# First phase of an adaLN attention and SwiGLU kernel: bias halves summed from PSUM, two zero-weight matmuls in a wait, K's first load between two weight loads

## The chip, the cores and the metric

The kernel runs on one core of one Trainium2 chip. The metric is the device time of one execution in microseconds (us). Each kernel was also profiled: the profile gives the span of the execution (first to last instruction, about 1.8 us shorter than the device time here), the busy time of each engine, and the clock granted to TensorE. Beside the time, each timed execution has its own span and its own mean granted clock, rounded to three decimals.

Engine names in the profile: PE is TensorE's matmuls, PEld its weight loads, DVE VectorE, ACT ScalarE, POOL GpSimd, SPq the queue that issues the loads. L1029 is a line of the kernel's source.

## The reference

```python
mod = (silu(c) @ w_mod)                # six vectors: sa, ca, ga, sb, cb, gb
h = layernorm(x) * (1 + ca) + sa       # x: 2048 x 1024
q = h @ wq                             # 32 heads of 128
s = q @ k.T * Dh ** -0.5               # last 512 keys, 4 kv heads
x = x + ga * (softmax(s) @ v) @ wo     # heads joined before wo
h = layernorm(x) * (1 + cb) + sb
x = x + gb * (silu(h @ w_gate) * (h @ w_up)) @ w_down
```

## The kernel before

The kernel works on blocks of 512 rows. All of the change lies in the first 35 us, where the first block's Q for heads 0 to 6 is made before the shift vector `sa` is there: Q is accumulated from the scaled input alone (`hs`), and what the shift adds to a head's Q, one column of 128 numbers, is made by matmuls whose `rhs` is a single column and added as a bias when Q is read from PSUM, where the kernel keeps the results of its matmuls. (In a matmul, `lhsT` is the weights; the columns of `rhs` are the last number of a timeline shape, 1 or 512.) All of these one-column results lie in one PSUM tile, `one_ps`: row 0 is the shift vector, rows 1 and 2 are the two halves of the bias.

```python
one_ps = mm("one_ps", (P, 3, 8))       # one PSUM tile

def q0(g, dts, src=None):              # Q of head g: matmuls of 512 columns
    for dt in dts:
        nc.tensor.matmul(q0_ps[g], lhsT=w0(g, dt),
                         rhs=hs[dt // 4][:, dt % 4, :] if src is None else src[:, dt, :],
                         start=(dt == 0), stop=(dt == DT - 1))

def sh_mm(half, heads):                # half of the bias: 4 one-column matmuls per head
    ...
            nc.tensor.matmul(one_ps[:, 1 + half, g:g + 1], lhsT=w0(g, dt),
                             rhs=sa_bf[:, dt:dt + 1], start=(i == 0), stop=(i == 3))

def sa_mm(half, tiles):                # shift vector: 8 one-column matmuls per tile
    ...
...
q0(3, (6, 7))
sh_mm(0, range(4))
q0(4, (6, 7))
sh_mm(0, range(4, H0))
...
nc.vector.tensor_copy(out=bias_q, in_=one_ps[:, 1, 0:H0])          # L1083
sa_mm(1, (0, 1))
q0(5, (6, 7))
sa_mm(1, (2, 3))
sa_out(1)                              # DVE reads the shift, casts it to bf16 (sa_bf)
q0(6, (6, 7))
sh_mm(1, range(H0))
...
nc.vector.tensor_tensor(out=bias_q, in0=one_ps[:, 2, 0:H0], in1=bias_q, op=ALU.add)   # L1094
q0_ps[H0] = mm("q_ps")                 # head 7 takes the bank of one_ps
q0(H0, range(DT), h10)
```

The loads go through one queue in program order: x, the modulation weights `wm`, `wq`, then the part that is changed:

```python
load_v(0)
load_wq(0, 2)                          # two loads of 512 KB, first used by head 8
load_kT(0)                             # K of kv head 0, transposed by the DMA
```

## Time and profile before

Three executions took 1273.43 to 1274.11 us, median 1273.8.

The page of the kernel before, its span, its busy times (share of the span, times the instructions) and the shares of the chain of waits that ended last:

```profile
span 1273.1 us, 18160 instructions
PE 1264.5 (99%) x7587; PEld 641.5 (50%) x7587; DVE 610.1 (48%) x1335; ACT 335.6 (26%) x440; POOL 1.3 (0%) x10
PE 97%; DVE 2%; DMA 0%; SPq 0%; issue 0%
```

PE is busy practically all the time and is the chain. So a delay of PE in the first phase is not hidden by anything later; it moves the end.

PE's rows of the timeline in that phase. The columns are start in us, busy us, engine, line, operation, what it writes and reads, shapes, how many, and in brackets how long the engine was idle before and what ended it. Rows of `128x1` are the one-column matmuls, rows of `128x512` the dense ones.

```profile
24.69 0.54 PE L1040 MATMUL one_ps<-sa_bf,wq 128*128 128x1 bf16 x16
25.09 0.59 PE L1029 MATMUL q_ps<-hs,wq 128*128 128x512 bf16 x2
25.52 0.44 PE L1040 MATMUL one_ps<-sa_bf,wq 128*128 128x1 bf16 x12
26.22 0.54 PE L1047 MATMUL one_ps<-siluc,wm 128*128 128x1 bf16 x16 [0.26 <-DVE bias_q L1083]
26.62 0.59 PE L1029 MATMUL q_ps<-hs,wq 128*128 128x512 bf16 x2
27.05 0.54 PE L1047 MATMUL one_ps<-siluc,wm 128*128 128x1 bf16 x16
27.45 0.59 PE L1029 MATMUL q_ps<-hs,wq 128*128 128x512 bf16 x2
28.05 0.84 PE L1040 MATMUL one_ps<-sa_bf,wq 128*128 128x1 bf16 x28
29.14 3.33 PE L1029 MATMUL q_ps<-hT,wq 128*128 128x512 bf16 x8 [0.26 <-DVE bias_q L1094]
32.26 1.32 PE L1190 MATMUL s_ps<-qT,kT 128*128 128x512 bf16 x4
...
36.25 1.07 PE L1222 MATMUL o_ps<-v_sb,pT 128*128 128x130 bf16 x16
```

Three things are to be seen. At 26.22 PE has waited for the DVE copy of the first bias half (L1083). At 29.14 it has waited for the second half (L1094), because head 7's Q takes the bank of `one_ps`. And the eight matmuls after that take 3.33 us, where eight such matmuls take 1.89 us later in the same trace.

The waits view of the window 22 to 32 us has the same two waits (total us, times, longest):

```profile
PE q_ps L1029 <- DVE bias_q L1094: 0.3, 1, 0.3
PE one_ps L1047 <- DVE bias_q L1083: 0.3, 1, 0.3
```

The windows view shows why the eight were slow. Its columns are the stretch, its length, the busy us of PE, PEld, DVE, ACT and POOL with their instructions, the granted clock of TensorE, the DMA share and GB/s:

```profile
22.60:26.02 3.42, 3.36 (x68) 2.25 (x67) 1.64 (x7) 0.00 (x0) 0.00 (x0) 1.00 1.12 325
26.02:29.43 3.41, 2.95 (x66) 2.12 (x66) 1.59 (x7) 1.54 (x3) 0.00 (x0) 1.00 1.95 157
29.43:32.84 3.41, 3.41 (x10) 1.24 (x9) 3.41 (x6) 1.12 (x2) 0.00 (x0) 0.50 1.02 189
32.84:36.26 3.42, 3.39 (x17) 1.37 (x16) 0.36 (x1) 3.08 (x4) 0.00 (x0) 1.00 0.18 50
```

The clock is 1.00, 1.00, then 0.50 for one stretch of 3.41 us, then 1.00 again. The cuts are set where the clock changes, and at multiples of 3.41 us from there.

| read from the profile of before | us |
|---|---|
| span | 1273.1 |
| PE stopped for `bias_q`, twice | 0.26 each |
| half-clock stretch | 29.43 to 32.84 |
| first one-column matmul to first `o_ps` matmul (22.86 to 36.25) | 13.39 |

The last row is the measure used below: it holds everything that the change touches on PE, and nothing of the loads of the start, whose arrival differs by about 1 us between executions (the first one-column matmul of this phase starts at 22.16 us in one trace below, that of real fill, and at 23.27 us in another, the second of before).

### The profile page before, as it was taken

The numbers are of one execution on the slowest core, as the hardware profiler recorded it, in microseconds if no ns is written. First come the engines' busy times: TensorE is split into PE (matmuls) and PEld (weight loads), VectorE is DVE, ScalarE is ACT, GpSimd is POOL, SyncE is SP. The second block draws the span as 40 slices with busy tenths as digits, with TensorE's granted clock in tenths as the row PEclk, the third lists the DMA queues.
The fourth block names the chain that finished last, engine by engine and source line by source line (L and its number), as shares of the span: only waits on it lengthen the run. The fifth ranks groups of instructions, "written<-read, shape, count | busy, mean of one in ns | idle before, by whom it ended". The sixth has DMA issues, their size and how long they took to land.

```text
span 1273.1 us, 18160 instructions
## 1 busy us (share of the span) xinstructions
PE 1264.5 (99%) x7587; PEld 641.5 (50%) x7587; DVE 610.1 (48%) x1335; ACT 335.6 (26%) x440; POOL 1.3 (0%) x10
## 2 busy tenths in 40 slices
PE   8999999999999999999999999999999999999998
PEld 4555555555555555555554444444444444444444
DVE  5666658885678665567564631321122112221122
ACT  3643334343333433334341111011100111011100
POOL 0000000000000000000000000000000000000000
PEclk9999999999999999999999999999999999999999
DMA  9897755878556655454575378326633566425702
GB/s 290 193 242 179 190 141 139 190 161 213 135 141 168 153 135 156 114 153 104 129 199 150 124 225 259 95 92 206 212 116 111 168 201 193 157 91 168 245 17 70
DMA packets 306844, 204.46 MB, mean 161 GB/s; under 512 B 145601, under 2 KB 303297, under 8 KB 306754
## 3 DMA queue, kind: packets, MB, share of 16 engines
q1 hardware_dynamic: 301842, 199.03, 57.8%
q10 hardware_dynamic: 4912, 4.20, 1.0%
q8 instruction: 61, 1.00, 0.3%
q14 instruction: 29, 0.24, 0.1%
HBM read 165.94 MB, written 4.21 MB: 134 GB/s over the span
## 4 chain that ended last, share of the span: by engine, by line
PE 97%; DVE 2%; DMA 0%; SPq 0%; issue 0%
PE gu_ps L1336 30%; PE a_ps L1254 17%; PE q_ps L1179 16%; PE d_ps L1356 15%; PE o_ps L1222 9%; PE s_ps L1190 8%; PE q_ps L1029 1%; DVE st L842 0%; DMA x<-in_A_x_dram 0%; DVE junk L1113 0%; DVE junk L813 0%; DVE oq L1209 0%; DVE qT L943 0%; DVE f L1267 0%; DVE f L1266 0%; DVE x L1269 0%
## 5 line engine op out<-in xcount | busy, mean ns | idle before, releaser
L1192 ACT ACTIVATE pT<-s_ps 128x1024 bf16<-128x1024 f32 x256 | 249.2, 1020 | 346.7 <-PE s_ps L1190 346.6
L1254 PE MATMUL a_ps<-wo,oT 128*128 128x512 bf16 x1024 | 241.9, 379 | 0.0
L1179 PE MATMUL q_ps<-hT,wq 128*128 128x512 bf16 x960 | 227.1, 379 | 0.0
L1342 DVE TENSOR_TENSOR guT<-gu_ps,sg 128x512 bf16<-128x512 f32 x112 | 77.5, 692 | 288.3 <-ACT sg L1341 288.3
L1336 PE MATMUL gu_ps<-hT,wg 128*128 128x512 bf16 x896 | 211.7, 379 | 0.0
L1341 ACT ACTIVATE sg<-gu_ps 128x512 bf16<-128x512 f32 x112 | 67.0, 598 | 488.5 <-PE gu_ps L1336 485.7
L1356 PE MATMUL d_ps<-wd,guT 128*128 128x512 bf16 (+2 forms) x952 | 194.2, 366 | 0.0
L1336 PE MATMUL gu_ps<-hT,wu 128*128 128x512 bf16 x672 | 163.3, 379 | 0.0
L1254 PEld LDWEIGHTS <-oT 128*128 128x128 bf16 x1024 | 100.2, 98 | 120.6
L943 DVE CAST qT<-q_ps 128x512 bf16<-128x512 f32 x121 | 83.6, 691 | 153.2 <-PE q_ps L1179 152.9
L1179 PEld LDWEIGHTS <-wq 128*128 128x128 bf16 x960 | 93.9, 98 | 113.0
L1356 PEld LDWEIGHTS <-guT 128*128 128x128 bf16 x952 | 90.9, 98 | 103.0
L1222 PEld LDWEIGHTS <-pT 128*128 128x128 bf16 x2048 | 126.6, 98 | 30.5 <-issue 0.4
L1336 PEld LDWEIGHTS <-wg 128*128 128x128 bf16 x896 | 87.6, 98 | 105.5
L1222 PE MATMUL o_ps<-v_sb,pT 128*128 128x130 bf16 x2048 | 137.0, 220 | 0.1
L1190 PE MATMUL s_ps<-qT,kT 128*128 128x512 bf16 x512 | 131.8, 380 | 0.0
L1336 PEld LDWEIGHTS <-wu 128*128 128x128 bf16 x672 | 65.7, 98 | 79.3
L1209 DVE TENSOR_TENSOR oq<-o_ps,rl 128x256 bf16<-128x256 f32 (+2 forms) x256 | 100.5, 420 | 3.9
L1360 DVE TENSOR_TENSOR f<-d_ps,gb_bc 128x512 f32<-128x512 f32 (+2 forms) x34 | 22.5, 660 | 140.8 <-PE d_ps L1356 140.8
L1190 PEld LDWEIGHTS <-kT 128*128 128x128 bf16 x512 | 45.1, 98 | 31.7 <-issue 1.3
L1262 DVE TENSOR_TENSOR acc<-a_ps,acc 128x512 f32<-128x512 f32 x64 | 44.0, 688 | 32.6 <-PE a_ps L1254 32.6
L1336 PE MATMUL gu_ps<-hT,v_sb 128*128 128x512 bf16 x224 | 57.5, 379 | 0.0
(97 smaller groups left out, 426.5 us busy)
## 6 DMA issues: line engine op xcount, KB each, us to landing
wq<-in_A_wq_dram SPq DMA_DIRECT2D x64, 512.0 KB
wo<-in_A_wo_dram SPq DMA_DIRECT2D x64, 512.0 KB
wg<-in_B_w_gate_dram SPq DMA_DIRECT2D x56, 512.0 KB
wd<-in_B_w_down_dram SPq DMA_DIRECT2D x56, 512.0 KB
wu<-in_B_w_up_dram SPq DMA_DIRECT2D x42, 512.0 KB
v_sb<-in_B_w_up_dram SPq DMA_DIRECT2D x14, 512.0 KB
x<-in_A_x_dram SPq DMA_DIRECT2D x16, 256.0 KB
wm<-in_w_mod_dram SPq DMA_DIRECT2D x4, 1024.0 KB
```

Of the source, the lines that this page charges most:

```text
L943: nc.vector.tensor_copy(out=t, in_=q_ps)
L1179: nc.tensor.matmul(q_ps, lhsT=w, rhs=hT[("h1", cc)][:, dt, :], start=(dt == 0), stop=(dt == DT - 1))
L1190: nc.tensor.matmul(s_ps[:, i, :], lhsT=kT[:, kv, j * P:(j + 1) * P], rhs=qT[g], start=True, stop=True)
L1192: nc.scalar.activation(out=p[:, 2 * jj:2 * jj + 2, :], in_=s_ps, func=ACT.Exp, scale=scale)
L1209: nc.vector.tensor_tensor(out=dst, in0=ps[:, s0:s0 + cnt, 0:Dh], in1=sc, op=ALU.mult)
L1222: nc.tensor.matmul(o_slot["ps"][:, s_, :], lhsT=pT[g][:, j, t * P:(t + 1) * P], rhs=v_sb[:, kv, j, 0:VN], start=(j == 0), stop=(j == WT - 1))
L1254: nc.tensor.matmul(a_ps, lhsT=oT[(cc, 2 * q + i)][:, hh % 4, t * P:(t + 1) * P], rhs=wo_tiles[(cc, q, dh, i)][:, hh % 4, :], start=(hh == ...
L1262: nc.vector.tensor_tensor(out=acc[(cc, t)][:, dsl], in0=a_ps, in1=acc[(cc, t)][:, dsl], op=ALU.add)
L1336: nc.tensor.matmul(ps[:, n, :], lhsT=gu_w[(cc, fg, nm, dt // 4)][:, dt % 4, fi * P:(fi + 1) * P], rhs=hT[("h2", cc)][:, dt, :], start=(dt ...
L1341: nc.scalar.activation(out=g, in_=ps[:, 0, :], func=ACT.Silu)
L1342: nc.vector.tensor_tensor(out=guT[(cc, fg)][:, fi, :], in0=ps[:, 1, :], in1=g, op=ALU.mult)
L1356: nc.tensor.matmul(d_ps, lhsT=guT[(cc, f // 4)][:, f % 4, t * P:(t + 1) * P], rhs=wd_tiles[(cc, dh, f // 4)][:, f % 4, c0:c0 + w], start=( ...
```

## The change

It means to take PE's two stops away and to keep its clock up. The bias halves are no longer copied one by one: one DVE reduce at the end sums both rows straight from PSUM, so PE need not wait in the middle. The one-column groups are dealt out differently between the dense pairs. Two dense matmuls with weights of zero, which add nothing to head 6's Q, run while DVE makes that sum. And K's first load goes between the two loads of `wq`, since scores will be wanted sooner.

```diff
-    load_wq(0, 2)
+    load_wq(0, 2, (0,))
     load_kT(0)
+    load_wq(0, 2, (1,))
...
+    zeros = const.tile([P, P], BF16, name="zeros")
+    nc.gpsimd.memset(zeros, 0.0)
...
-                             start=(dt == 0), stop=(dt == DT - 1))
+                             start=(dt == 0), stop=(dt == DT - 1 and g != H0 - 1))
...
-    sh_mm(0, range(4))
+    sh_mm(0, range(5))
     q0(4, (6, 7))
-    sh_mm(0, range(4, H0))
+    sh_mm(0, (5, 6))
...
-    nc.vector.tensor_copy(out=bias_q, in_=one_ps[:, 1, 0:H0])
-    sa_mm(1, (0, 1))
+    sa_mm(1, (0,))
     q0(5, (6, 7))
-    sa_mm(1, (2, 3))
+    sa_mm(1, (1, 2, 3))
     sa_out(1)
-    q0(6, (6, 7))
+    q0(H0 - 1, (6,))
+    q0(H0 - 1, (7,))
     sh_mm(1, range(H0))
+
+    for i in range(2):
+        nc.tensor.matmul(q0_ps[H0 - 1], lhsT=zeros, rhs=warm_w, start=False, stop=(i == 1))
...
-    nc.vector.tensor_tensor(out=bias_q, in0=one_ps[:, 2, 0:H0], in1=bias_q, op=ALU.add)
+    nc.vector.tensor_reduce(out=bias_q, in_=one_ps[:, 1:3, 0:H0].rearrange("p a g -> p g a"),
+                            axis=AX.X, op=ALU.add)
```

## The prediction

> **What bounds it.** TensorE. The page gives PE 99% busy over 1273.1 us, and the chain that ended last is 97% PE. From 33 us on the windows view shows PE busy nearly all the time, so what moves the first head's dense work moves the end by as much.
>
> **Where time is lost there (timeline, PE rows).**
> 1. At 25.98 PE stops until 26.22: it may not write `one_ps` before DVE has copied `bias_q` (L1083). The next 16 one-column matmuls take 0.54 us, against 0.38 in the chain elsewhere: 0.24 + 0.16 = 0.40 us.
> 2. At 28.90 it stops until 29.14: the bank that head 7's Q needs is read last by the second `bias_q` (L1094).
> 3. The windows view shows the granted clock at 0.50 in 29.43 to 32.84 and 1.00 around it. 512-column matmuls start there every 0.427 us instead of 0.215; eight lose 8 x 0.21 = 1.7 us. [...] the slow stretch is 3.41 us long, and the equal stretch before it (26.02 to 29.43) is the thinnest: about 1.15 us of 512-column streaming (5.3 x 0.215), against about 1.55 in the stretch before, which kept the clock.
>
> **What the change does.**
> - Bias halves summed straight from PSUM: removes wait 1 (-0.40 us) and a DVE copy of 0.17 us (off the path); the final reduce should take about the 0.17 us of the add it replaces.
> - Two zero matmuls: +0.43 us on PE, into wait 2, where 0.24 us of idle and 0.16 of restart vanish: about 0.
> - Reordering moves one-column work, removes none. Dense streaming starts near 28.5 (zero matmuls), head 7's Q near 28.9. The stretch 26.02 to 29.43 then holds about 1.8 us of streaming, more than the 1.55 that kept the clock. So no half clock: -1.5 to -1.7 us.
> - K's first transpose lands about 30.4 in the trace, and scores started at 32.26. With a faster PE scores want it near 30.65; issued 1.5 us earlier it lands near 29. Worth nothing itself; it keeps the gain from becoming a DMA wait. The second `wq` half lands later, but is first used near 32.5.
> - The zeros memset (POOL) is off the path.
>
> **On the critical path:** 0.2 to 0.4 us of waits and up to 1.7 us of clock, less some 0.2 us because ACT's 0.97 us exponentials pace the first two heads. First `o_ps` matmul at about 34.4 instead of 36.25; the shift stays to the end. Sum: -1.8 us, 0.14%.
>
> **Prediction:** 1272.0 us, range 1270.9 to 1273.3. Faster by over 2%: 0.5%; within 2%: 99%; slower by over 2%: 0.5%.
>
> **What would show it.** Granted clock 1.00 throughout 20 to 40 us; no PE row waiting for `bias_q`; head 7's eight Q matmuls in about 1.9 us instead of 3.33; scores starting near 30.7 without waiting for `kT`.
>
> **What would make it wrong.** [...] in another phase a thin stretch (24.7 to 28.1 holds about 1.3 us even after the change) may still trip it, leaving only 0.3 us; or the timed runs of before did not all pay it. Scores may wait for `kT` or ACT. Run to run noise is 0.7 us, near the effect's size.

-0.40 us for the first wait, about 0 for the zero matmuls, -1.5 to -1.7 us for the clock and some 0.2 us back for ACT came to -1.8 us. The clock term was the estimate from one trace, in which a stretch with 1.15 us of dense work was followed by the half clock and one with 1.55 us was not. In the last paragraph, "another phase" is another place of these 3.41 us stretches, and what a thin stretch may "trip" is the clock.

## The result, and the profile after

The changed kernel took 1272.92 to 1273.72 us, median 1273.02 of 6 executions; the kernel before, 1273.43 to 1274.63, median 1273.98 of 6. The ratio is 0.9993, with a 95% interval of 0.998 to 1.0006. A ratio here is the mean time of one kernel's runs over that of the other's of the same rounds, so it is not quite the ratio of the medians. 0.96 us of 1274 is far under 2%, and the interval holds 1. The profiled span is 1271.2 us, 1.9 us under that of before.

The page after, the lines that answer to those of before:

```profile
span 1271.2 us, 18164 instructions
PE 1263.8 (99%) x7589; PEld 641.3 (50%) x7589; DVE 609.8 (48%) x1334; ACT 335.6 (26%) x440; POOL 1.4 (0%) x11
PE 97%; DVE 2%; DMA 0%; SPq 0%; issue 0%
```

PE's rows of the timeline after (columns as above; L1032 is the dense Q, L1043 the bias, L1050 the shift vector, L1095 the zero matmuls):

```profile
24.80 0.64 PE L1043 MATMUL one_ps<-sa_bf,wq 128*128 128x1 bf16 x20
25.30 0.59 PE L1032 MATMUL q_ps<-hs,wq 128*128 128x512 bf16 x2
25.73 0.34 PE L1043 MATMUL one_ps<-sa_bf,wq 128*128 128x1 bf16 x8
25.93 0.34 PE L1050 MATMUL one_ps<-siluc,wm 128*128 128x1 bf16 x8
26.13 0.59 PE L1032 MATMUL q_ps<-hs,wq 128*128 128x512 bf16 x2
26.56 0.74 PE L1050 MATMUL one_ps<-siluc,wm 128*128 128x1 bf16 x24
27.16 0.59 PE L1032 MATMUL q_ps<-hs,wq 128*128 128x512 bf16 x2
27.76 0.84 PE L1043 MATMUL one_ps<-sa_bf,wq 128*128 128x1 bf16 x28
28.46 0.59 PE L1095 MATMUL q_ps<-warm_w,zeros 128*128 128x512 bf16 x2
28.89 1.89 PE L1032 MATMUL q_ps<-hT,wq 128*128 128x512 bf16 x8
30.61 1.03 PE L1197 MATMUL s_ps<-qT,kT 128*128 128x512 bf16 x4
...
34.31 1.07 PE L1229 MATMUL o_ps<-v_sb,pT 128*128 128x130 bf16 x16
```

No row waits for `bias_q` any more. The zero matmuls start at 28.46, head 7's eight Q matmuls take 1.89 us and not 3.33, and the first `o_ps` matmul starts at 34.31 instead of 36.25. From the first one-column matmul (22.96) to there it is 11.35 us, against 13.39.

The windows view after, cut at multiples of 3.41 us from this execution's first rise of the clock (7.21 us):

```profile
24.27:27.69 3.42, 3.42 (x71) 2.20 (x69) 1.94 (x9) 0.10 (x1) 0.00 (x0) 1.00 1.25 217
27.69:31.10 3.41, 3.41 (x42) 1.92 (x41) 3.09 (x8) 2.57 (x4) 0.00 (x0) 1.00 1.40 186
31.10:34.51 3.41, 3.38 (x19) 1.50 (x18) 1.72 (x3) 3.27 (x4) 0.00 (x0) 1.00 0.71 120
```

The clock is 1.00 in all of them. From the first `o_ps` matmul to the end it is 1236.86 us after and 1236.89 before (span less start): nothing later was gained or lost.

So the two traces differ by 1.97 us of span and agree with the predicted 1.8 almost step by step. The timed medians differ by 0.96 us only. The experiments were made to find where the other half is.

### The profile page after: what moved, and what is told of

Same layout as the page of the kernel before. It is cut to its first block, busy times and chain, and to the rows that moved or that the text cites. A ratio compares the mean times of both kernels' runs of the same rounds, so it can differ in the third digit from the quotient of the medians.

```text
span 1271.2 us, 18164 instructions
## 1 busy us (share of the span) xinstructions
PE 1263.8 (99%) x7589; PEld 641.3 (50%) x7589; DVE 609.8 (48%) x1334; ACT 335.6 (26%) x440; POOL 1.4 (0%) x11
## 4 chain that ended last, share of the span: by engine, by line
PE 97%; DVE 2%; DMA 0%; SPq 0%; issue 0%
PE gu_ps L1343 30%; PE a_ps L1261 17%; PE q_ps L1186 16%; PE d_ps L1363 15%; PE o_ps L1229 9%; PE s_ps L1197 8%; PE q_ps L1032 1%; DVE st L845 0%; DMA x<-in_A_x_dram 0%; DVE junk L1120 0%; DVE junk L816 0%; DVE oq L1216 0%; DVE qT L946 0%; DVE f L1274 0%; DVE f L1273 0%; DVE x L1276 0%
```

## The experiments

Two theories. The clock theory, a guess from the trace of before (3.41 us at clock 0.50 after a stretch of 3.41 us with 1.15 us of dense work): the half clock follows a stretch, from here on a window, of 3.41 us that held too little streaming by dense matmuls; where the windows lie differs from one execution to the next, so the kernel before pays that in a part of its executions, and the changed kernel in none. The waits-only rival: the gain is that of the two stops, and the half clock has nothing to do with what the change does.

"Streaming" below is worked out from the timeline: 0.215 us, the start to start distance of 512-column matmuls at full clock, for each such matmul, as far as it lies in the window; the recorded starts are taken as the starts of streaming. Some records are missing (rows of `x1` where the kernel has pairs); they are added, one each in the windows below of sum alone and of zeros alone. In the traces, 512-column matmuls start 0.427 us apart at half clock and 0.215 us at full clock, one-column matmuls 0.025 us apart.

Mean clocks of 0.998 are read below as executions with one half-clock window in the middle, those of 0.999 or 1.0 as executions without: the trace of before, with one, has 0.998, that of after, without, 1.0. (3.41 us at half clock take 0.0013 from the mean; in these two traces the clock also falls for the last 1.26 and 1.03 us, which takes 0.0005 and 0.0004.) A reading near the edge of rounding can mislead for a single run; for the kernel before the times agree with it: its ten runs with 0.998 took 1274.43 us or more, and of its 31 others one took more than 1274.1 (1274.52).

### The parts alone

**Sum from PSUM alone.**

```diff
-    nc.vector.tensor_copy(out=bias_q, in_=one_ps[:, 1, 0:H0])
...
-    nc.vector.tensor_tensor(out=bias_q, in0=one_ps[:, 2, 0:H0], in1=bias_q, op=ALU.add)
+    nc.vector.tensor_reduce(out=bias_q, in_=one_ps[:, 1:3, 0:H0].rearrange("p a g -> p g a"),
+                            axis=AX.X, op=ALU.add)
```

> Only the first part: the two bias halves are summed by one reduce from PSUM, no copy of the first half; order of before, no zero matmuls, old DMA order. Both theories: the stop of PE at 25.98 us is gone, head 7's Q starts 0.40 us sooner (28.74 instead of 29.14). Clock theory: the stretch before Q stays thin (two pairs of 512-column matmuls and about 0.2 us of a third, 1.1 us of streaming in the thinnest 3.41 us), so half-clock windows still occur in some or most executions: times spread over some 1.5 us, median 0.4 us under before. Waits-only theory (the half clock has nothing to do with the thin stretch): 0.4 us under before, and half-clock windows as often as in the changed kernel.

Measured: 1273.04 to 1274.93, median 1274.07 of 5; before, in the same session, 1272.81 to 1275.06, median 1273.47 of 9. Two of the five runs have clock 0.998, and two of the nine of before. The 0.4 us under before that both theories expected is not seen in the medians, which depend on how many half clocks fell on each side. The trace happened to be one with a half clock: 13.09 us from the first one-column matmul to the first `o_ps` matmul, 0.30 less than the 13.39 of before, also at half clock. The stop in the middle is gone; the expected 0.40 fell short by 0.1, probably because the second half of the shift weights landed only at 26.00 us by the DMA's completion events; PE's next one-column matmul started at 26.05. The windows view:

```profile
25.94:29.35 3.41, 3.07 (x72) 2.24 (x71) 1.65 (x7) 1.62 (x3) 0.00 (x0) 1.00 1.59 137
29.35:32.76 3.41, 3.41 (x10) 1.18 (x8) 3.41 (x6) 1.04 (x2) 0.00 (x0) 0.50 1.50 153
```

The thin window held 1.22 us of streaming and brought the half clock.

**Zero matmuls alone.**

```diff
+    zeros = const.tile([P, P], BF16, name="zeros")
+    nc.gpsimd.memset(zeros, 0.0)
...
     sh_mm(1, range(H0))
+    for i in range(2):
+        nc.tensor.matmul(q0_ps[H0 - 1], lhsT=zeros, rhs=warm_w, start=False, stop=(i == 1))
```

> Only the two zero matmuls, everything else as before. Both theories: PE's stop at 28.90 us is filled; the zero matmuls cost 0.43 us and save 0.24 of idle and 0.16 of restart, so Q of head 7 starts at about 29.33 and ends where it would have at full clock (within 0.05 us). Clock theory: dense streaming starts 0.24 us sooner than in before, the thinnest 3.41 us holds about 1.05 to 1.1 us instead of 0.87: half-clock windows become rarer but do not vanish; median 0.3 to 1 us under before. Waits-only theory: no change of time (within 0.1 us).

Measured: 1273.37 to 1274.99, median 1273.56 of 5; one run has clock 0.998. By time alone, no difference from before that these runs could show; the 0.3 to 1 us that the clock theory expected is not there. The trace is worth more: the clock window fell in the same place as in the run above (25.93), and the clock stayed up:

```profile
25.93:29.35 3.42, 3.08 (x73) 2.21 (x71) 1.52 (x8) 1.34 (x2) 0.00 (x0) 1.00 1.99 188
29.35:32.76 3.41, 3.38 (x17) 1.44 (x16) 3.41 (x6) 2.42 (x5) 0.00 (x0) 1.00 0.95 176
```

PE's busy time in the two thin windows is the same within 0.01 us (3.07 and 3.08); what differs is streaming, 1.22 against 1.34 us, of which 0.43 are the zero matmuls. So matmuls with weights of zero count for the clock as other dense ones do, as far as this trace shows: without them the window would hold 0.91 us, less than the 1.22 us after which the clock fell. At full clock this kernel needs 11.74 us for the measured stretch.

**Everything but the zero matmuls** (the two-line loop taken out of the changed kernel, and the `stop` flag put back).

> The changed kernel without the two zero matmuls (sum from PSUM, new order and new DMA order stay). Both theories: Q of head 7 starts at about 28.75 after a PE stop of 0.24 us and 0.16 us of restart; at full clock the same time as the changed kernel within 0.05 us. Clock theory: the thinnest 3.41 us holds about 1.2 us instead of 1.3 (and 1.2 to 1.3 in a wider range of phases), so some executions have a half-clock window and are 1 to 1.7 us longer; spread over 1 us. Waits-only theory: same times and same spread as the changed kernel.

Measured: 1272.73 to 1274.73, median 1273.39 of 5; one run (the 1274.73) has clock 0.998, the others 0.999 or 1.0. The trace, at full clock, needs 11.31 us, the changed kernel 11.35. So at full clock the zero matmuls gain nothing that can be seen: the difference of 0.04 us is less than that between traces of one kernel (the changed kernel's three need 11.35, 11.36 and 11.48). What they are good for is the clock.

**One-column matmuls in the place of the dense zero ones.**

```diff
-    for i in range(2):
-        nc.tensor.matmul(q0_ps[H0 - 1], lhsT=zeros, rhs=warm_w, start=False, stop=(i == 1))
+    for i in range(17):
+        nc.tensor.matmul(q0_ps[H0 - 1][:, 0:1], lhsT=zeros, rhs=warm_w[:, 0:1], start=False, stop=(i == 16))
```

> The changed kernel with the two 512-column zero matmuls replaced by 17 zero matmuls of one column (17 x 25 ns = 0.43 us): PE is as busy and never stops, but streams 0.43 us less. This separates filling the wait from streaming. Clock theory [...]: dense work starts at 28.9 instead of 28.5, the thinnest 3.41 us holds about 1.1 us, half-clock windows come back in some executions, which are 1 to 1.7 us longer than the others. Waits-only theory: time and spread equal to the changed kernel (within 0.1 us).

Measured: 1272.64 to 1274.93, median 1273.12 of 5; one run (1274.93) has clock 0.998, the others are at 1273.31 or less. The trace, at full clock, needs 11.34 us. Filling the wait costs the same with either kind. With one-column matmuls a half clock still comes, in one run of five.

### The kernel before in another phase, and the changed kernel again

> The kernel before, unaltered, for a trace in another phase of the clock window and for the count of its slow-clock executions. Clock theory: about a quarter of executions have the half clock (clock 0.998, span about 1273.0). If this trace falls in another phase (3 in 4), it shows full clock between 20 and 40 us and the time from the first one-column group to the first o_ps matmul is 11.7 to 11.8 us, not 13.39: 0.4 us over the changed kernel's 11.35, and span about 1271.6. Rival (the half clock belongs to every execution of the kernel before, as my prediction assumed): 13.4 us again and clock 0.998 in all runs.

Measured: 1272.99 to 1274.73, median 1273.57 of 5; one run has clock 0.998 (1274.73). Beside it, in the nine runs of before of that session, two have 0.998 (1275.02 and 1274.97), the other seven are 1273.30 to 1273.66. The trace is one at full clock. Its windows:

```profile
24.20:27.61 3.41, 3.15 (x74) 2.21 (x72) 1.78 (x7) 0.00 (x0) 0.00 (x0) 1.00 1.35 314
27.61:31.03 3.42, 3.16 (x54) 1.89 (x50) 2.64 (x8) 2.67 (x4) 0.00 (x0) 1.00 1.48 106
31.03:34.44 3.41, 3.38 (x16) 1.46 (x15) 2.48 (x4) 2.54 (x3) 0.00 (x0) 1.00 0.86 155
```

And three of PE's rows in it, head 7's Q after the wait, the first scores, the first output:

```profile
29.55 1.89 PE L1029 MATMUL q_ps<-hT,wq 128*128 128x512 bf16 x8 [0.26 <-DVE bias_q L1094]
31.27 1.03 PE L1190 MATMUL s_ps<-qT,kT 128*128 128x512 bf16 x4
...
34.97 1.07 PE L1222 MATMUL o_ps<-v_sb,pT 128*128 128x130 bf16 x16
```

The unaltered kernel before, with both its stops, needs 11.70 us here, not 13.39. The thin window held 1.29 us of streaming and passed. So one form of the rival fails, the one that my prediction shared: the half clock does not belong to every execution of the kernel before.

> The changed kernel again, unaltered, to count its executions with a half-clock window beside the others on the same chip. Clock theory: the thinnest 3.41 us of it holds about 1.3 us of streaming; two traces bracket the threshold (1.22 us tripped, 1.34 us did not), so none or at most one of five runs shows clock 0.998; the rest 1272.6 to 1273.4 us. Waits-only theory: 0.998 as often as in the kernel before (2 of 9 runs in the last session).

Measured: 1272.65 to 1273.33, median 1272.87 of 5, no clock of 0.998. Before in that session: 1273.16 to 1274.76, median 1273.89 of 9, two with 0.998. The trace needs 11.36 us.

> The changed kernel once more, beside the two others on the same chip. No run with clock 0.998; median 1272.7 to 1273.1 us.

Measured: 1272.46 to 1273.77, median 1273.22 of 5, no clock of 0.998. The median is a little over what was expected. The trace needs 11.48 us.

All runs of the two kernels that have a clock of their own, over all sessions (so over several chips):

| | runs | with clock 0.998 | mean of those, us | mean of the others, us |
|---|---|---|---|---|
| before | 41 | 10 | 1274.85 | 1273.49 |
| after | 16 | 0 | - | 1273.04 |

If the clock reading had nothing to do with the change, none in 16 beside 10 in 41 would come about by chance in some 3 of 100 cases. Where the clock stayed up, the change is worth 1273.49 - 1273.04 = 0.45 us (give or take 0.2), about the 0.35 us by which the traces differ at full clock (11.70 against 11.35). An execution of before with a half-clock window is 1.36 us longer than one without. Ten of 41 have one: 0.24 x 1.36 = 0.33 us on the average. The sum, 0.78 us (give or take 0.3), is what the change gains on the average. In the three sessions that ran both kernels the means differ by 0.90, 1.01 and 0.73 us.

### Thin against dense, with the same time on PE

To see the clock without luck, the wait was made much longer than it needs to be, once with one-column matmuls and once with dense ones, each about 2.15 us.

**86 one-column zero matmuls** (as the 17 above, with 86).

> The changed kernel with 86 one-column zero matmuls (86 x 25 ns = 2.15 us) in place of the two of 512 columns: PE issues without a stop but streams almost nothing for 2.8 us. Both theories: 2.15 - 0.43 = 1.72 us more PE time than the changed kernel. Clock theory: nearly every phase of the window now has a thin window, so nearly all five runs show clock 0.998 and are 1.2 to 1.7 us longer still: about 3.0 to 3.4 us over the changed kernel, and as much as 1.2 to 1.7 us over the next kernel. Waits-only theory: equal to the next kernel.

**Ten dense zero matmuls** (`range(10)` in place of `range(2)`).

> The changed kernel with ten 512-column zero matmuls (10 x 0.215 = 2.15 us) in place of two: the same PE time as the run with 86 one-column matmuls, but all of it streaming. Both theories: 1.72 us over the changed kernel. Clock theory: none of five runs shows clock 0.998. Waits-only theory: as often as the run with one-column matmuls.

Measured: 1277.41 us median (1277.21 to 1277.8, 5 runs) with 86 thin ones, all five with clock 0.998 or 0.997; 1274.67 us median (1274.3 to 1274.83, 5 runs) with ten dense ones, all five with clock 1.0. The dense kernel is 1.80 us over the changed kernel of the session (1272.87), as its PE time says (1.72). The thin kernel is 2.74 us over the dense one, more than the 1.2 to 1.7 expected. Part of that was not foreseen: its trace has a stop of 0.63 us after the 60th of the 86 matmuls (with the 28 of the bias before them, the 88th in a row) for which the profile names no cause ("issue"); its cause is open. That left a gap in the argument: the stop, and not the thin streaming, might have halved the clock. So one more run.

**50 one-column zero matmuls.**

> The changed kernel with 50 one-column zero matmuls (50 x 25 ns = 1.25 us) in place of the two of 512 columns. The run with 86 of them had a stop of PE of 0.63 us among them, so it did not separate thin streaming from a stop; 50 should pass without one. Both theories: 1.25 - 0.43 = 0.82 us over the changed kernel. Streaming theory: windows that start 25.35 to 27.1 us after the start hold less than 1.25 us of streaming, half of all phases; so 1 to 4 of 5 runs have clock 0.998 and are about 1.5 us longer than the others (about 1275.4 against 1273.9). Rival (a stop of PE, not thin streaming, brings the half clock): no run of five with clock 0.998, all near 1273.9 us.

Measured: 1275.78, 1275.12 and 1274.97 with clock 0.998, 1273.93 and 1273.72 with clock 1.0: three of five. The trace is one of the three. Its thin window and the one after:

```profile
26.19:29.61 3.42, 3.42 (x106) 2.78 (x103) 1.75 (x7) 1.78 (x3) 0.00 (x0) 1.00 1.54 235
29.61:33.02 3.41, 3.41 (x27) 1.48 (x24) 2.84 (x5) 0.88 (x2) 0.00 (x0) 0.50 0.91 160
```

PE was busy in all 3.42 us of the first window, with 106 matmuls and without a stop, and still the clock was halved in the next. Dense matmuls filled 0.86 us of it. Two rows of the timeline show the fifty, and the eight dense ones at half clock after them:

```profile
28.69 1.41 PE L1095 MATMUL q_ps<-warm_w,zeros 128*128 128x1 bf16 x50
29.96 3.38 PE L1032 MATMUL q_ps<-hT,wq 128*128 128x512 bf16 x8
```

The rival that a stop brings the half clock is out. With the 86 and the ten (five of five against none of five), this also refutes the waits-only rival in what it says of the half clock: the same PE time brings one or not according to what fills it. That the two stops are part of the gain is so; by the pooled means they are 0.45 of 0.78 us.

The windows of the traces, put in order of streaming:

| kernel | window, us | streaming, us | clock of the next window |
|---|---|---|---|
| 86 one-column | 28.45 to 31.87 | 0.57 | 0.50 |
| 50 one-column | 26.19 to 29.61 | 0.86 | 0.50 |
| before | 26.02 to 29.43 | 1.15 | 0.50 |
| sum alone | 25.94 to 29.35 | 1.22 | 0.50 |
| before, second trace | 24.20 to 27.61 | 1.29 | 1.00 |
| zeros alone | 25.93 to 29.35 | 1.34 | 1.00 |
| after | 24.27 to 27.69 | 1.64 | 1.00 |

They divide between 1.22 and 1.29 us, 36 to 38% of the window. The other windows of the two traces of before and after, from the first rise of the clock on, fit if matmuls of 128 to 256 columns are counted too, by their columns (0.215 us for 512): the clock fell only once more in each, at the kernel's end (1271.88 and 1270.14 us), after a window with no matmul in it, and never after one with 1.55 us or more, which is all the others. By 512-column matmuls alone they would not: one window of before (8.95 to 12.37 us) held 0.92 us of those and kept the clock, beside 24 matmuls of 128 columns. PE's busy time does not divide them (3.42 us in the run with 50 lost the clock, 3.08 in zeros alone kept it), nor does that of the weight loads (2.12 us in before lost it, 2.21 in zeros alone kept it, 2.24 in sum alone lost it). With a limit of 1.25 us, put between the measured 1.22 and 1.29, one can estimate from the starts in the timeline which places of the window are bad. For the kernel before these are starts from 25.13 to 26.12 us, 0.99 of 3.41 us or 29% of all phases; 10 of 41 runs is 24%. For the kernel with 50 one-column matmuls it is 52%; it was three of five. For the changed kernel the thinnest 3.41 us hold three pairs, 1.29 us: no phase is bad; 0 of 16 runs. For the four kernels under "The parts alone" it gives 15 to 20%; 5 of their 20 runs have clock 0.998. The two of them that have all but the dense zeros have 2 in 10 against 0 in 16, too few to show by counting alone that the zeros are needed. All of these shares are estimates: the limit is nothing but the middle between two of the seven windows in the table, and the margin of 0.04 us is small.

### The order of the loads

```diff
-    load_wq(0, 2, (0,))
-    load_kT(0)
-    load_wq(0, 2, (1,))
+    load_wq(0, 2)
+    load_kT(0)
```

> The changed kernel with the old order of loads (both weight halves, then K). If moving K matters: K's first transpose lands at 30.4 to 31.4 us (as in four traces with the old order or with a late start), scores are wanted at 30.6, so PE waits 0 to 0.7 us before the first score matmul in the trace, and the median is 0 to 0.5 us above the changed kernel. If it does not matter: K lands before 30.6, no wait, times equal.

Measured: 1272.54 to 1273.83, median 1273.07 of 5, no clock of 0.998; the changed kernel in the same session had 1272.87. By the DMA's completion events K's first load landed at 30.16 us, and the first score matmul started at 30.21, as in the changed kernel's trace of that session. PE lost 0.03 us (from head 7's Q to the scores 1.75 us, against 1.72 in that other trace), and the weight load of K waited for the DMA (total us, times, longest):

```profile
PEld L1196 <- DMA kT<-in_A_k_cache_dram: 0.4, 1, 0.4
```

In the other traces with the old order K landed at 30.38, 30.49, 30.69 and 31.37 us; with the new order at 27.33 to 28.13. The changed kernel wants it at 29.93 to 30.61. So the old order leaves a margin of 0.05 us here, and a later landing would have been a longer wait, but no run shows one. Whether the moved load is worth anything on the average stays open: 1273.12 against 1272.90 us (means of five) is within the spread.

### Real work in the place of the zeros

If dense matmuls are wanted in the two waits, real ones would do. Here four of head 6's own Q matmuls are held back: two for the wait for the shift, two for the place of the zeros, which are gone.

```diff
-    for g in range(H0):
+    for g in range(H0 - 1):
         q0(g, (4, 5))
...
-    q0(H0 - 1, (6,))
-    q0(H0 - 1, (7,))
+    q0(H0 - 1, (4, 5))
     sh_mm(1, range(H0))
-    (the two zero matmuls)
+    q0(H0 - 1, (6, 7))
```

> The changed kernel without zero matmuls: four of head 6's real Q matmuls are kept back instead, two fill the wait for the bias before its second half, two the wait after it. PE does 0.43 us less. If the waits are filled as well as by zeros and the loads of the shift weights come in time (they are wanted 0.43 us sooner, and landed 0.3 to 0.9 us ahead in most traces), the time from the first dense Q matmul to the first o_ps matmul is 0.43 us shorter than the changed kernel's 22.2, no half clock (thinnest 3.41 us still about 1.3 us), median 0.2 to 0.45 us under the changed kernel. If the loads set the pace: equal to the changed kernel.

Measured: 1272.51 to 1273.35, median 1272.77 of 5, no clock of 0.998; the changed kernel beside it had a median of 1273.22 with a spread of 1.3 us. The traces decide: from the first dense Q matmul to the first `o_ps` matmul this kernel takes 22.34 us and the changed kernel of the session 22.31. The 0.43 us of zeros saved were lost to the loads: 0.30 us in the wait below, and about 0.1 us at the second landing. The waits view of that trace:

```profile
PE one_ps L1048 <- DMA wm<-in_w_mod_dram: 0.3, 1, 0.3
```

The shift weights land at 22.11 and 25.21 us, and PE cannot start on them sooner. This execution had an early start (first dense Q at 11.31 us, like the changed kernel's in that session at 11.32, where the other traces have 11.7 to 12.4), so with a later start the loads might not limit it; that was not seen. It is not shown to beat the changed kernel.

## Why the prediction was right or wrong

The time: 1273.02 us was measured, within the range of 1270.9 to 1273.3 and within 2%, but the expected gain was 1.8 us and the measured one 0.96. That the number lies in the range is in part luck: the largest term of the sum was counted at some five times its average weight, and the number fits only because the range reached down to a gain of 0.5 us.

- "Bias halves summed straight from PSUM: removes wait 1 (-0.40 us)". Right. Between zeros alone and the changed kernel, both at full clock, there are 11.74 - 11.35 = 0.39 us; new order and sum together (traces of the changed kernel differ by up to 0.13). The DVE reduce took 0.17 us, as predicted.
- "Two zero matmuls: +0.43 us on PE, into wait 2 [...]: about 0". Right: 11.35 against 11.31 us.
- "So no half clock: -1.5 to -1.7 us". This is the step that was mis-sized. Right for an execution that would have had the half clock: at almost the same place of the window, the trace of before took 13.39 us and that of zeros alone 11.74. Wrong as a term of the median: it counted with full weight what happens in about a quarter of the executions (10 of 41). The trace that I read was one of that quarter, and the record of that execution says so (its span of 1273.1 us, which the prediction quotes, did too): it took 1275.01 us with clock 0.998, and the 1.8 us read from it were taken off 1273.8, the median of three other executions. Taken off 1275.01 they give 1273.2, near the 1273.02 measured; the two profiled executions differ by 2.00 us. On the average the term is 0.33 us and not 1.6. The prediction named this ("the timed runs of before did not all pay it") but put it among the risks and not in the sum.
- The 0.2 us that the sum took off because ACT paces the first two heads did not show: the traces of before and after differ by 2.04 us up to the first `o_ps` matmul, the sum without that deduction.
- The sum with the right weight, worked out afterwards: 0.35 at full clock and 0.33 for the clock, 0.7 us. Measured: 0.78 from the pooled means, 0.96 between the first medians.
- The predicted places in the trace held: the zero matmuls at 28.46 (predicted 28.5), head 7's Q at 28.89 (28.9), scores at 30.61 (30.65), the first `o_ps` at 34.31 (34.4). The streaming of the thinnest part, 1.3 us, was right; the risk named for it did not come about: no clock of 0.998 in 16 runs, and in the second trace of before a window with 1.29 us kept the clock.
- "K's first transpose [...] lands near 29": it landed at 27.46. That the move itself is worth nothing in the median agrees with the run (1273.07 against 1272.87, within the spread), but that it was needed is not shown.
- The place of the 3.41 us windows. The half-clock stretch of the trace of before is 3.41 us long, and the full-clock stretches before and after it are whole multiples of that (23.89 and 1239.04 us, 7 and 363 windows). With the first matmul at 1.60 us in both traces, the clock first rose at 5.54 us in that of before and at 7.21 us in that of after. So the place of the windows is not tied to the first matmul; the prediction named another phase as a risk but did not carry it into the arithmetic.

## What to carry to other kernels

Before a trace is read, its own time and clock should be set beside those of the timed executions (here 1275.01 us and 0.998 beside 1273.8): a gain read from a slower execution must not be taken off the median of others. A single trace shows one place of the clock's windows (first rise at 5.54 us in one trace here, at 7.21 us in another); before a loss seen in it is booked as gain, its frequency over executions is to be counted, here from the granted clock of each run (10 of 41). After stretches of one-column matmuls the dense work can run at half clock (0.50 in these traces), even if TensorE never stops (three of five runs with 50 of them); mixing dense matmuls in, even with zero weights and in a wait that is there anyway, kept the clock in all 16 runs here, at a cost too small to be seen here (11.35 against 11.31 us). And where a wait is to be filled with real work moved from earlier, look first whether the loads allow everything to move up.
